# Local q and k loaded as rows of nine tokens, transposed by token pairs, and another order of the attention parts

## The chip, the cores and the metric

The kernel runs on one core of a Trainium2 chip. The metric is the device time of one execution in microseconds (us); less is better. The engines are TensorE (PE, with PEld for its weight loads), VectorE (DVE), ScalarE (ACT), GpSimd (POOL) and SyncE (SP), which issues all the DMAs here. TensorE's clock has two levels, 1.2 and 2.4 GHz; the profile gives the granted clock as a share of the upper one, so 0.50 is 1.2 GHz and 1.00 is 2.4 GHz.

## The reference

Three layers are chained, in fp32 (the MLP weights arrive as 64-bit floats).

```python
# attention: B=4, H=8, S=576, D=64; heads 0-3 local, heads 4-7 strided
rel = pos[:, None] - pos[None, :]
mask_local   = (rel >= 0) & (rel < 32)
mask_strided = (rel >= 0) & (pos[None, :] % 32 == pos[:, None] % 32)
attn = softmax(where(mask, q @ k.T / 8, -1e9)) @ v
x = attn.transpose(0, 2, 1, 3).reshape(2304, 512)
# soft mixture of 8 experts, 4 slots each: w1 (8,512,1024), w2 (8,1024,512)
logits = x @ phi
slot_in = softmax(logits, axis=0).T @ x
slot_out = relu(slot_in @ w1) @ w2          # expert by expert
x = softmax(logits, axis=1) @ slot_out
# MLP: w_in (512,2048), w_out (2048,512)
h = relu(x @ w_in)
out = (h * h) @ w_out
```

## The kernel before, in words

**Stages.** The attention part works on 16 units (`units`, L340): one batch and one pair of heads each, in the order of heads (0,1), (4,5), (2,3), (6,7), so that even units are local and odd units strided. After each four units (one batch) the logits and a running sum of the slot inputs are made (`L`, `R1`, `R2`, `R3`). `st_end` (L815) closes the attention stage. Then come the expert layers (`layer1` L1025, `layer2` L1048), in which 64 weight blocks of 512 KB are used, and then the MLP, whose inner product (L1229) fills the rest of the time.

**Parts of a unit.** `ld` (L368) loads q and k of a unit into one of NR = 3 raw buffers; `lv` (L392) loads v, and for a local unit `vs` (L407) copies v shifted by a block with two POOL copies (L410). `Tk` and `Tq` (`st_T`, L496) transpose k and q on PE into PSUM banks; `k` (L532) and `q` (L518) copy them out of the banks, q with the scale. `S` (L545) makes the scores, `s` (L583) subtracts the maximum on DVE, `e` (L608) takes the exponential on ACT, `n` (L612) normalises strided units, `PT` (L624) transposes the probabilities, `p` (L638) copies them out, `A` (L655) multiplies with v, `a` (L679) copies that out, `X` (L701) transposes the result and `x` (L711) copies it out.

**Order.** `PIPE` (L30) lists the parts of one iteration by hand, one list for even and one for odd units; a token's number is the lag (`A-1` is the part A of the unit before). `emit` (L921) walks through it. PE, ACT, DVE and POOL keep that order (`pin`, L100), one queue each. SP is not pinned: it issues a DMA in an order that the scheduler chose, each once its buffer is free, but a weight's DMA stays behind the last q/k load that was emitted before it (`pace`, L115).

**Local q and k before.** A local unit's q (and k) is loaded by three DMAs (L379 twice, L390): four tiles of 128 tokens for each of two heads and a rest of 64 tokens. Each token is a piece of 64 floats, 256 B. PE makes four transposes (L501) and one product with 64 columns of the identity (L503); the banks then hold tokens in order, and q leaves them by one ACT instruction (L525), k by two ACT copies of 64 partitions (L537, recorded at the helper's line L488). A strided unit's q and k come in pieces of 1024 B and 512 B (L385, L390).

**Weights.** `fetch` (L266) starts loads of expert and MLP weights into a ring of RING = 27 slots of 512 KB, and later into the 16 parts of the attention's own memory (`space`) as `give` (L299) hands them over when a unit's part was the last one to use it. The token `ft` starts `PACE` (L34) of them: 1 in an even and 2 in an odd iteration of the first half, 4 in an even and 0 in an odd one of the second half, 28 in all. `cv` converts one fetched w_in block. When all of `space` is given, `fetch` starts whatever still fits.

**Filling products.** `F1` and `DRAIN` (L25) put products without a use on PE (`fill_last`, L148, recorded at L153), one instruction each; `KEEP` does so in `st_end` (L824).

**Copies.** `ON_ACT` (L35) says which of a part's copies go to ACT (1) or DVE (0); for `n`, 2 means POOL.

Of the kernel before, what the change touches and what calls it, by code (L numbers as in the profile page):

```python
# [12 lines left out]
ALU = mybir.AluOpType  # L13
# [7 lines left out]
NA = 16  # L21
SPARE = 0
AHEAD = 4
KEEP = (4, 0, 0, 8, 0)
DRAIN = dict(S0=0, PT1=0, A1=3, X1=4, PT0=1, A0=1)  # L25
LATE = 3

PIPE = (  # L30
    "PT-1 p-1 lv+0 S+0 x-3 Tk+1 ft s+0 Tq+1 L-2 R2 vs+0 R3 ld+3 q+1 X-2 e+0 R1 n+0 cv F1 ld+4 A-1 lv+1 x-2 k+1 F1 F1 F1 a-1".split(),
    "PT-1 p-1 S+0 s+0 cv Tq+1 ft e+0 n+0 Tk+1 A-1 L-2 a-1 R2 k+1 vs+0 R1 X-2 q+1 R3".split(),
)
PACE = (1, 2, 4, 0)  # L34
ON_ACT = dict(kL=(1, 1), kS=(1, 1), pL=1, pS=(0, 0), xL=0, xS=1, aS=(1, 1, 1, 0), q=1, n=2)  # L35

@with_exitstack
def kernel(
# [119 lines left out]
    def flat(ps):  # L158
        return ps.rearrange("p b c -> p (b c)")
# [183 lines left out]
    ends = {}  # L343
    raws = {}
    for u in range(NU - NR, NU):
        raws[u % NR] = [part(128, 8 * D) for _ in range(2)] + [part(128, 2 * D)]
        ends["T", u] = at[0]
    qTl, kTl = part(128, S), part(128, 2, 32 + S)
    ends["S", NU - 2] = at[0]
# [13 lines left out]
    def local(u):  # L363
        return units[u][1] < 2

    raw = {}

    def load(u):  # L368
        if u >= NU:
            return  # L370
        b, p = units[u]
        raw[u] = raws[u % NR]
        r = raw[u][2]
        for n, src in ((1, k), (0, q)):
            i = src[b, 2 * p:2 * p + 2]
            m = raw[u][n]
            if local(u):
                for h in range(2):
                    nc.sync.dma_start(  # L379
                        out=m.rearrange("p (t h d) -> p t h d", h=2, d=D)[:, :, h],  # L380
                        in_=i[h, 0:512].rearrange("(t p) d -> p t d", p=128),
                    )
                o, i = r[64 * n:64 * n + 64].rearrange("p (h d) -> p h d", h=2), i[:, 512:576].rearrange("h p d -> p h d")
            else:
                nc.sync.dma_start(  # L385
                    out=m.rearrange("p (h x) -> p h x", h=2),
                    in_=i[:, 0:512].rearrange("h (p r) d -> p h (r d)", r=4),
                )
                o, i = r[64 * n:64 * n + 64], i[:, 512:576].rearrange("h (p e) d -> p h (e d)", e=2)
            pace[0] = nc.sync.dma_start(out=o, in_=i)  # L390
# [16 lines left out]
    def shift_v(u):  # L407
        if local(u):
            for h in range(2):
                nc.gpsimd.tensor_copy(  # L410
                    vL[64 * h:64 * h + 32, 1:18, h, 0:D], vL[64 * h + 32:64 * h + 64, 0:17, h, 0:D]
                )

# [51 lines left out]
    nc.vector.tensor_copy(masks, ms)  # L465
    for e in range(2):
        nc.vector.memset(kTs[ts(e, 64), :, 1 - e], 0.0)
    for h in range(2):
        nc.vector.memset(vL[ts(h, 64), :, 1 - h], 0.0)
    for h in range(2):  # L470
        nc.vector.memset(Ts[ts(h, 64), :, 2 - 2 * h:4 - 2 * h], 0.0)
    for t in (vS, Ps):
        behind(nc.gpsimd.memset(t, 0.0), last_diag)
    load_v(1)
# [2 lines left out]
    for t in El:  # L477
        behind(nc.gpsimd.memset(t[:, 192:256], 0.0), last_diag)
    shift_v(0)
    nc.gpsimd.tensor_copy(phi4[:, :, 1:4], phi4[:, :, 0:1].to_broadcast([128, KD, 3, NS]))  # L480
    nc.vector.tensor_reduce(
        out=sub2, in_=ident.rearrange("p (i c) -> p c i", c=2), axis=AX.X, op=ALU.add
# [11 lines left out]
        return ps  # L494

    def st_T(ps, u, n):  # L496
        m, r = raw[u][n], raw[u][2]
        pf = flat(ps)
        w = 128 if local(u) else 256
        for t in range(4):  # L500
            nc.tensor.transpose(out=pf[:, w * t:w * t + 128], in_=m[:, ts(t, 128)], identity=ident)  # L501
        if local(u):
            nc.tensor.matmul(out=pf[:, 512:576], lhsT=r, rhs=ident[:, ts(n, 64)], start=True, stop=True)  # L503
            return
        for h in range(2):
            nc.tensor.matmul(  # L506
                out=ps[:, h].rearrange("c (j x) -> c x j", j=2)[:, 128:144],
                lhsT=r, rhs=ident[:, ts(n, 64)].rearrange("k (p h) -> k h p", h=2)[:, h],
                start=True, stop=True,
            )  # L510

    def blocks(ps):
        return flat(ps).rearrange("c (n x) -> c n x", n=4)[:, :, 0:144]

    def st_Tq(u):
        st_T(hold("q", u), u, 0)

    def st_q(u):  # L518
        ps = held.pop(("q", u))
        if local(u):  # L520
            o, i = qTl, flat(ps)[:, 0:S]
        else:
            o, i = qTs, blocks(ps)
        if ON_ACT["q"]:
            nc.scalar.activation(out=o, in_=i, func=AF.Copy, scale=scale)  # L525
        else:
            nc.vector.tensor_scalar(out=o, in0=i, scalar1=scale, scalar2=None, op0=ALU.mult)

    def st_Tk(u):
        st_T(hold("k", u), u, 1)  # L530
# [1 line left out]
    def st_k(u):  # L532
        ps = held.pop(("k", u))
        i = blocks(ps)
        if local(u):
            for h in range(2):
                copy(ON_ACT["kL"][h], kTl[ts(h, 64), h, 32:32 + S], flat(ps)[ts(h, 64), 0:S])  # L537
        else:
            for e in range(2):
                copy(  # L540
                    ON_ACT["kS"][e], kTs[ts(e, 64), :, e].rearrange("c (b y) i -> c b y i", y=8),
                    i[ts(e, 64)].rearrange("c b (i y) -> c b y i", y=8),
                )

# [67 lines left out]
    def st_n(u):  # L612
        if local(u):
            return
        P = Pe.rearrange("p n (w s) -> p n w s", s=2)
        sm = ap_.tile([128, 8, 2], F32, tag="sm", name="sm", bufs=2)
        nc.vector.tensor_reduce(out=sm, in_=P.rearrange("p n w s -> p n s w"), axis=AX.X, op=ALU.add)
        nc.vector.tensor_scalar(out=sm, in0=sm, scalar1=1e-9, scalar2=None, op0=ALU.add)
        nc.vector.reciprocal(out=sm, in_=sm)
        (nc.gpsimd if ON_ACT["n"] == 2 and u < NU - 1 else nc.vector).tensor_tensor(  # L620
            out=P, in0=P, in1=sm[:, :, None, :].to_broadcast([128, 8, 18, 2]), op=ALU.mult
        )

# [14 lines left out]
    def st_p(u):  # L638
        pf = flat(held.pop(("p", u)))
        if local(u):  # L640
            copy(ON_ACT["pL"], Tl[:, 0:S], pf[:, 0:S])
        else:
            i = pf[:, 0:512].rearrange("p (n w) -> p n w", w=32)[:, :, 0:18]
            for h in range(2):
                r = ts(h, 64)
                if ON_ACT["pS"][h]:
                    for s in range(2):
                        nc.scalar.activation(out=Ts[r, :, 2 * h + s], in_=i[r], func=AF.Copy, scale=sub2[r, s:s + 1])
                else:
                    nc.vector.tensor_tensor(  # L650
                        out=Ts[r, :, 2 * h:2 * h + 2], in0=i[r, :, None, :].to_broadcast([64, 16, 2, 18]),
                        in1=sub2[r, None, :, None].to_broadcast([64, 16, 2, 18]), op=ALU.mult,
                    )
# [25 lines left out]
    def st_a(u):  # L679
        ps = held.pop(("a", u))  # L680
        if local(u):
            x = xNs[u] = xNb[:, u % 5]
            pv = flat(ps)[:, 122:772].rearrange("p (n e) -> p n e", e=65)
            den = ap_.tile([128, 10], F32, tag="den", name="den", bufs=2)
            nc.vector.tensor_scalar(out=den, in0=pv[:, :, D], scalar1=1e-9, scalar2=None, op0=ALU.add)
            nc.vector.reciprocal(out=den, in_=den)
            nc.vector.tensor_tensor(
                out=x.rearrange("p t (h d) -> p (t h) d", h=2), in0=pv[:, :, 0:D],
                in1=den[:, :, None].to_broadcast([128, 10, D]), op=ALU.mult,
            )  # L690
        else:
            xT = xTs[u] = xTb[u % 4]
            for h in range(2):
                for x in range(2):
                    copy(
                        ON_ACT["aS"][2 * h + x],
                        xT[ts(h, 64), 0:S].rearrange("c (i x k n) -> c x i k n", x=2, k=2, n=4)[:, x],
                        ps[ts(x, 64), :, 0:288].rearrange("c k (h i n) -> c h i k n", h=2, n=4)[:, h],
                    )
# [11 lines left out]
    def st_x(u, act=None):  # L711
        pf = flat(held.pop(("x", u)))
        if local(u):
            xT = xTs[u] = xTb[u % 4]
            copy(ON_ACT["xL"], xT[:, 0:S], pf[:, 0:S])
        else:
            x = xNs[u] = xNb[:, u % 5]
            copy(ON_ACT["xS"] if act is None else act, x, pf[:, 0:640].rearrange("p (t f) -> p t f", f=128))

    lps = {}  # L720

# [199 lines left out]
    def emit(u, token):  # L921
# [362 lines left out]
```

## Time and profile before

| what | us |
|---|---|
| median of 3 runs (413.55 to 416.15) | 415.74 |
| the profiled execution, whole | 418.53 |
| its span, first to last instruction | 416.8 |
| attention stage, to the first expert product (L1030) | 147.9 |
| expert layers, to the first product of the slots' sum (L1076) | 181.7 |

Times within the trace count from the span's start. The profiled execution lasted 1.7 us more than its span and 2.8 us more than the median. Over the span PE was busy 93%, DVE 58%, ACT 54%, POOL 22%.

### The profile page before, as it was taken

The page shows a single profiled execution, that of the slowest core. Times are in us where ns is not written, and L with a number is a line of the kernel's source. Part 1 is how long each engine was busy: PE and PEld are TensorE (multiplying, and loading weights), DVE is VectorE, ACT ScalarE, POOL GpSimd, SP SyncE. Part 2 cuts the span into 40 slices and gives each one's busy share as a digit, 9 for nine tenths or more (in the row PEclk, how much of TensorE's full clock was granted, in tenths as well). Part 3 has the DMA queues.
Part 4 walks back from the last instruction along what each step waited for, and adds up shares of the span by engine and source line. Part 5 has one row for each costly group of instructions (what it writes and reads, how often), then busy time and mean ns, then how long its engine had stood idle before and what let it go on. Part 6 is the DMA issues. An engine that isn't in the chain of part 4 may idle for free.

```text
span 416.8 us, 9152 instructions
## 1 busy us (share of the span) xinstructions
PE 387.3 (93%) x3654; PEld 302.3 (73%) x3654; DVE 242.6 (58%) x453; ACT 226.7 (54%) x459; POOL 90.8 (22%) x128
## 2 busy tenths in 40 slices
PE   6887798889699899999999999999999999999996
PEld 3776576777587645467788887888887888878884
DVE  6565547765265561138866564867657776745434
ACT  3452627536345220039778686666666676666760
POOL 6302211112022020035600252111414103420000
PEclk9998979999799999999999999999999999999999
DMA  6898898998999999997212131221000000003033
GB/s 153 234 251 227 215 227 300 210 293 203 274 384 270 395 333 417 417 417 309 87 64 102 51 103 58 95 101 50 2 0 1 2 0 2 1 0 153 37 116 151
DMA packets 52203, 69.88 MB, mean 168 GB/s; under 512 B 31744, under 2 KB 37120, under 8 KB 52160
## 3 DMA queue, kind: packets, MB, share of 16 engines
q1 hardware_dynamic: 52160, 69.29, 52.2%
q8 instruction: 29, 0.48, 0.5%
q14 instruction: 14, 0.11, 0.1%
HBM read 64.55 MB, written 4.72 MB: 166 GB/s over the span
## 4 chain that ended last, share of the span: by engine, by line
PE 73%; DMA 9%; DVE 5%; POOL 4%; ACT 3%; SPq 3%; issue 2%; POOLq 0%; DVEq 0%; ACTq 0%
PE banks L1229 43%; DMA space<-in_v_dram 6%; PE banks L1060 4%; PE banks L1190 4%; PE banks L1030 3%; PE banks L501 2%; DMA w<-in_moe_w_dram 2%; PE banks L554 2%; PE banks L1120 2%; PE banks L665 1%; PE banks L673 1%; POOL w L1105 1%; PE banks L728 1%; PE banks L734 1%; POOL space L410 1%
## 5 line engine op out<-in xcount | busy, mean ns | idle before, releaser
L1229 PE MATMUL banks<-w 128*128 128x512 f32 x864 | 218.3, 394 | 1.6 <-POOL w L1105 1.2
L1229 PEld LDWEIGHTS banks<-w 128*128 128x128 f32 x864 | 159.3, 188 | 37.2 <-POOL w L1105 2.9
L1206 DVE TENSOR_TENSOR w<-r,w 128x384 fp32r<-128x384 f32 (+1 forms) x97 | 57.8, 598 | 72.4 <-ACT w L1205 72.3
L1197 ACT ACTIVATE r<-banks 128x384 f32<-128x384 f32 (+1 forms) x96 | 47.0, 490 | 53.0 <-PE banks L1190 43.6
L1203 ACT ACTIVATE r<-r 128x384 f32<-128x384 f32 (+1 forms) x96 | 50.3, 524 | 3.0
L1205 ACT CAST w<-r 128x384 fp32r<-128x384 f32 (+1 forms) x97 | 49.5, 510 | 4.1 <-DVE r L1202 0.5
L488 ACT COPY space<-banks 64x576 f32<-64x576 f32 (+2 forms) x64 | 34.8, 543 | 19.5 <-PE banks L153 12.2
L220 POOL TENSOR_SCALAR nm<-w 128x512 f32<-128x512 f32 x28 | 23.5, 843 | 63.0 <-DMA w<-in_moe_w_out_dram 31.9
L1244 DVE TENSOR_TENSOR part<-banks,part 128x512 f32<-128x512 f32 (+1 forms) x55 | 34.9, 673 | 2.4 <-PE banks L1229 2.3
L410 POOL COPY space<-space 32x1088 f32<-32x1088 f32 x16 | 17.5, 1096 | 80.9 <-DMA space<-in_v_dram 57.6
L1104 POOL CAST w<-wf 128x512 fp32r<-128x512 f32 x16 | 11.8, 740 | 94.8 <-PE banks L1229 37.2
L1190 PE MATMUL banks<-cT,A 128*128 128x384 f32 x96 | 32.0, 335 | 0.0
L501 PE MATMUL banks<-ident,space 128*128 128x128 f32 x128 | 21.9, 297 | 1.6 <-DMA space<-in_q_dram 1.6
L224 DVE SCALAR_TENSOR_TENSOR nm<-w,nm 128x512 uint32<-128x512 uint32 x32 | 22.3, 696 | 1.1
L223 DVE TENSOR_SCALAR nm<-nm 128x512 uint32<-128x512 uint32 x32 | 14.6, 457 | 12.5 <-POOL nm L220 8.7
L1105 POOL TENSOR_TENSOR w<-wf,w 128x512 fp32r<-128x512 f32 x16 | 21.4, 1339 | 1.4
L525 ACT ACTIVATE space<-banks 128x576 f32<-128x576 f32 x16 | 10.4, 651 | 20.1 <-PE banks L506 15.9
L1190 PEld LDWEIGHTS banks<-cT,A 128*128 128x128 f32 x96 | 18.0, 188 | 3.9 <-ACT r L1197 0.2
L488 DVE COPY space<-banks 128x576 f32<-128x576 f32 (+1 forms) x16 | 9.7, 608 | 17.3 <-ACT space L488 13.5
L501 PEld LDWEIGHTS banks<-ident,space 128*128 128x128 f32 x128 | 15.7, 159 | 4.7 <-POOL w L437 2.5
L665 PE MATMUL banks<-space 128*32 128x130 f32 x288 | 13.0, 294 | 5.6 <-POOL space L410 3.7
L665 PEld LDWEIGHTS banks<-space 128*32 128x32 f32 x288 | 9.5, 116 | 7.7 <-POOL space L410 4.7
(186 smaller groups left out, 450.4 us busy)
## 6 DMA issues: line engine op xcount, KB each, us to landing
w<-in_moe_w_dram SPq DMA_DIRECT2D x48, 512.0 KB, 7.3
w<-in_moe_w_in_dram SPq DMA_DIRECT2D x16, 512.0 KB
space<-in_moe_w_dram SPq DMA_DIRECT2D x16, 512.0 KB, 7.4
w<-in_moe_w_out_dram SPq DMA_DIRECT2D x16, 512.0 KB, 6.6
space<-in_v_dram SPq DMA_DIRECT2D x32, 144.0 KB, 7.5
out_dram<-part SPq DMA_DIRECT2D x17, 256.0 KB, 2.0
space<-in_k_dram SPq DMA_DIRECT2D x16, 128.0 KB, 2.9
space<-in_q_dram SPq DMA_DIRECT2D x16, 128.0 KB, 2.6
```

The lines of the kernel that those rows point to most:

```text
L220: nc.gpsimd.tensor_scalar(out=m, in0=hf, scalar1=2.0 ** -112, scalar2=1.0, op0=ALU.mult, op1=ALU.mult)
L488: return (nc.scalar.copy if act else nc.vector.tensor_copy)(out=out, in_=in_)
L501: nc.tensor.transpose(out=pf[:, w * t:w * t + 128], in_=m[:, ts(t, 128)], identity=ident)
L665: nc.tensor.matmul(out=pv[c, n // 4] if n < 18 else pv[c, 4].rearrange("p (h e) -> p h e", h=2), lhsT=w, rhs=i, start=True, stop=True, til ...
L1105: nc.gpsimd.tensor_tensor(out=lo, in0=r, in1=hi.bitcast(F32), op=ALU.subtract)
L1190: nc.tensor.matmul(out=ps[:, 0:HB], lhsT=A4[c][:, ts(f % QF, 128)], rhs=cT4[:, c0:c0 + HB], start=True, stop=True)
L1197: nc.scalar.activation(out=r[:, cuts[0]], in_=ps[:, cuts[0]], func=AF.Relu)
L1203: nc.scalar.activation(out=r[:, cuts[0]], in_=r[:, cuts[0]], func=AF.Square)
L1205: nc.scalar.copy(out=gh[:, x], in_=r[:, x])
L1206: nc.vector.tensor_tensor(out=gl[:, x], in0=r[:, x], in1=gh[:, x].bitcast(F32), op=ALU.subtract)
L1229: nc.tensor.matmul(out=acc[t], lhsT=a[:, ts(t, 128)], rhs=wo[f][:, ts(w, 512)], start=(first and k == 0), stop=(last and k == 2),)
L1244: nc.vector.tensor_tensor(out=pt[:, cs], in0=acc[t][:, cs], in1=pt[:, cs], op=ALU.add)
```

## The change

A local unit's q (and k) is loaded by one DMA, each of 128 partitions taking nine consecutive tokens of one head, one piece of 2304 B. PE transposes two tokens at a time (four transposes of 128 columns and one of 64); tokens then lie out of order in the banks, even ones of nine on partitions 0 to 63 and odd ones on 64 to 127, and four copies of 64 partitions ("quarters", two of 320 and two of 256 elements) put them in order, writing every ninth element. The order of the parts, the fetch counts, the engines of the copies (now apart for the first two units, `_b`, and the last two, `_e`) and the filling products change too; `n`'s product goes from POOL to DVE for units 2 to 13, the first unit's `Tk k Tq q` are emitted ahead, and four clearings of memory go from DVE to POOL.

```diff
-KEEP = (4, 0, 0, 8, 0)
-DRAIN = dict(S0=0, PT1=0, A1=3, X1=4, PT0=1, A0=1)
+KEEP = (4, 0, 0, 8, 3)
+DRAIN = dict(S0=3, PT1=0, A1=4, X1=8, PT0=0, A0=0)
 PIPE = (
-    "PT-1 p-1 lv+0 S+0 x-3 Tk+1 ft s+0 Tq+1 L-2 R2 vs+0 R3 ld+3 q+1 X-2 e+0 R1 n+0 cv F1 ld+4 A-1 lv+1 x-2 k+1 F1 F1 F1 a-1".split(),
-    "PT-1 p-1 S+0 s+0 cv Tq+1 ft e+0 n+0 Tk+1 A-1 L-2 a-1 R2 k+1 vs+0 R1 X-2 q+1 R3".split(),
+    "vs+0 Tq+1 PT-1 x-3 p-1 q+1 S+0 s+0 R2 ft L-2 Tk+1 cv k+1 R1 X-2 e+0 R3 x-2 A-1 ld+3 ld+4 n+0 lv+1 F1 a-1".split(),
+    "S+0 s+0 Tk+1 e+0 cv k+1 PT-1 Tq+1 p-1 R2 R3 A-1 ft vs+0 n+0 L-2 X-2 a-1 q+1 lv+1 R1".split(),
 )
-PACE = (1, 2, 4, 0)
-ON_ACT = dict(kL=(1, 1), kS=(1, 1), pL=1, pS=(0, 0), xL=0, xS=1, aS=(1, 1, 1, 0), q=1, n=2)
+PACE = (0, 2, 4, 0)
+ON_ACT = dict(kL=(1, 1, 1, 1), qL=(1, 1, 1, 1), kS=(1, 1), pL=0, pS=(0, 0), xL=0, xS=1, aS=(1, 0, 1, 1), q=1, n=0, vs=(0, 0), kL_b=(1, 1, 1, 1), qL_b=(0, 0, 0, 1), kL_e=(0, 1, 0, 1), qL_e=(0, 0, 1, 1), ...)
@@ load
-            if local(u):
-                for h in range(2):
-                    nc.sync.dma_start(
-                        out=m.rearrange("p (t h d) -> p t h d", h=2, d=D)[:, :, h],
-                        in_=i[h, 0:512].rearrange("(t p) d -> p t d", p=128),
-                    )
-                o, i = r[64 * n:64 * n + 64].rearrange("p (h d) -> p h d", h=2), i[:, 512:576].rearrange("h p d -> p h d")
...
+            if local(u):
+                todo_ = [(raw[u][:, ts(n, 9 * D)], i.rearrange("h (x r) d -> (h x) (r d)", r=9))]
@@ constants
-    for h in range(2):
-        nc.vector.memset(vL[ts(h, 64), :, 1 - h], 0.0)
-    for h in range(2):
-        nc.vector.memset(Ts[ts(h, 64), :, 2 - 2 * h:4 - 2 * h], 0.0)
...
     shift_v(0)
+    for h in range(2):
+        nc.gpsimd.memset(vL[ts(h, 64), :, 1 - h], 0.0)
+    for h in range(2):
+        nc.gpsimd.memset(Ts[ts(h, 64), :, 2 - 2 * h:4 - 2 * h], 0.0)
@@ st_T
+        if local(u):
+            m = raw[u][:, ts(n, 9 * D)]
+            for w in range(5):
+                c = min(128, 9 * D - 128 * w)
+                nc.tensor.transpose(out=pf[0:c, ts(w, 128)], in_=m[:, 128 * w:128 * w + c], identity=ident)
+            return
@@ st_q, st_k
+    def quarters(t, ps):
+
+        for h in range(2):
+            for e in range(2):
+                o = (t[ts(h, 64), h] if len(t.shape) == 3 else t[ts(h, 64)]).rearrange("c (x r) -> c r x", r=9)
+                i = flat(ps)[ts(e, 64), 0:640].rearrange("c (w h x) -> c h w x", w=5, h=2)
+                yield 2 * h + e, o[:, e:9:2], i[:, h, 0:5 - e]
-            o, i = qTl, flat(ps)[:, 0:S]
+            todo_ = [(on("qL", u)[n], o, i) for n, o, i in quarters(qTl, ps)]
-            for h in range(2):
-                copy(ON_ACT["kL"][h], kTl[ts(h, 64), h, 32:32 + S], flat(ps)[ts(h, 64), 0:S])
+            for n, o, x in quarters(kTl[:, :, 32:32 + S], ps):
+                copy(on("kL", u)[n], o, x)
@@ the loop over the units
+    for token in ("Tk+1", "k+1", "Tq+1", "q+1"):
+        emit(-1, token)
     for u in range(-1, NU + 3):
         for token in PIPE[u % 2]:
             emit(u, token)
```

## Rows read from the trace of the kernel before

**Rows 1.** The page's 40 slices, GB/s that the DMA engines moved.
```profile
GB/s 153 234 251 227 215 227 300 210 293 203 274 384 270 395 333 417 417 417 309 87 64 102 51 103 58 95 101 50 2 0 1 2 0 2 1 0 153 37 116 151
```
**Rows 2.** Windows: length, busy us of five engines, granted clock, DMA share, GB/s.
```profile
0.00:10.00 10.00, 6.28 (x21) 3.45 (x21) 6.02 (x18) 2.75 (x4) 6.22 (x27) 1.00 0.66 152
10.50:98.20 87.70, 74.67 (x1381) 60.99 (x1381) 52.17 (x103) 41.83 (x84) 17.06 (x27) 0.94 0.92 240
98.20:147.90 49.70, 42.96 (x736) 34.72 (x730) 26.78 (x63) 20.37 (x48) 6.84 (x7) 0.93 1.01 322
147.90:177.00 29.10, 29.10 (x362) 13.37 (x365) 8.29 (x14) 4.11 (x6) 2.23 (x4) 1.00 0.99 388
51.30:58.10 6.80, 6.80 (x61) 5.51 (x63) 2.69 (x7) 1.88 (x6) 0.00 (x0) 0.50 0.99 306
109.30:116.10 6.80, 5.56 (x107) 4.91 (x108) 0.79 (x2) 1.82 (x4) 2.13 (x2) 0.50 1.11 274
```
**Rows 3.** The chain that ended last: start us, us, what.
```profile
10.50 2.04 PE banks L554 x33
...
23.07 8.96 DMA space<-in_v_dram
...
34.48 2.37 PE banks L665 x35
...
147.90 7.04 PE banks L1030 x64
...
181.69 0.84 PE banks L1076 x8
```
**Rows 4.** Waits from 0 to 150 us: waiting line, what ended it, us, times, longest.
```profile
PE banks L673 <- DMA space<-in_v_dram: 3.9, 2, 3.7
PE banks L665 <- POOL space L410: 3.7, 3, 1.4
...
PE banks L634 <- POOL space L620: 2.2, 2, 1.3
...
PE banks L629 <- ACT space L488: 2.0, 3, 1.0
...
PE banks L665 <- DMA space<-in_v_dram: 1.9, 2, 1.4
```
**Rows 5.** Timeline of SP's DMA issues: start us, us, line, transfer, count.
```profile
0.81 0.99 SPq L379 DMA_DIRECT2D space<-in_k_dram  x2
...
3.79 0.61 SPq L390 DMA_DIRECT2D space<-in_q_dram  x1
...
148.93 20.66 SPq L120 DMA_DIRECT2D w<-in_moe_w_dram  x21
```
**Rows 6.** The page's DMA issues: transfer, count, KB each, median us to landing.
```profile
w<-in_moe_w_dram SPq DMA_DIRECT2D x48, 512.0 KB, 7.3
```
**Rows 7.** Groups by shape, 0 to 180 us: busy us, mean ns, idle before.
```profile
L501 PE MATMUL banks<-ident,space 128*128 128x128 f32 x128 | 21.9, 297 | 1.6 <-DMA space<-in_q_dram 1.6
L488 ACT COPY space<-banks 64x576 f32<-64x576 f32 x32 | 20.2, 631 | 6.9 <-PE banks L503 6.4
...
L525 ACT ACTIVATE space<-banks 128x576 f32<-128x576 f32 x16 | 10.4, 651 | 20.1 <-PE banks L506 15.9 <-DVE space L589 4.0
...
L488 ACT COPY space<-banks 64x288 f32<-64x288 f32 x24 | 9.5, 394 | 12.4 <-PE banks L153 12.2
...
L503 PE MATMUL banks<-ident,space 128*128 128x64 f32 x32 | 5.7, 263 | 0.0
...
L153 PE MATMUL banks<-maskl,identb 128*128 128x384 bf16 x17 | 4.6, 327 | 0.0
...
L488 DVE COPY space<-banks 64x288 f32<-64x288 f32 x8 | 3.7, 461 | 15.7 <-ACT space L488 13.5 <-PE banks L734 2.1
...
L447 DVE MEMSET space<- 64x32 f32 x2 | 0.2, 85 | 0.1
...
L449 DVE MEMSET space<- 64x18 f32 x2 | 0.1, 73 | 0.0
```

More of the change, by code (lines that the diff above doesn't have):

```diff
@@ L23 @@
 AHEAD = 4
-KEEP = (4, 0, 0, 8, 0)
-DRAIN = dict(S0=0, PT1=0, A1=3, X1=4, PT0=1, A0=1)
+KEEP = (4, 0, 0, 8, 3)
+DRAIN = dict(S0=3, PT1=0, A1=4, X1=8, PT0=0, A0=0)
 LATE = 3
 PIPE = (
-    "PT-1 p-1 lv+0 S+0 x-3 Tk+1 ft s+0 Tq+1 L-2 R2 vs+0 R3 ld+3 q+1 X-2 e+0 R1 n+0 cv F1 ld+4 A-1 lv+1 x-2 k+1 F1 F1 F1 a-1".split(),
-    "PT-1 p-1 S+0 s+0 cv Tq+1 ft e+0 n+0 Tk+1 A-1 L-2 a-1 R2 k+1 vs+0 R1 X-2 q+1 R3".split(),
-)
-PACE = (1, 2, 4, 0)
-ON_ACT = dict(kL=(1, 1), kS=(1, 1), pL=1, pS=(0, 0), xL=0, xS=1, aS=(1, 1, 1, 0), q=1, n=2)
+    "vs+0 Tq+1 PT-1 x-3 p-1 q+1 S+0 s+0 R2 ft L-2 Tk+1 cv k+1 R1 X-2 e+0 R3 x-2 A-1 ld+3 ld+4 n+0 lv+1 F1 a-1".split(),
+    "S+0 s+0 Tk+1 e+0 cv k+1 PT-1 Tq+1 p-1 R2 R3 A-1 ft vs+0 n+0 L-2 X-2 a-1 q+1 lv+1 R1".split(),
+)
+PACE = (0, 2, 4, 0)
+ON_ACT = dict(kL=(1, 1, 1, 1), qL=(1, 1, 1, 1), kS=(1, 1), pL=0, pS=(0, 0), xL=0, xS=1, aS=(1, 0, 1, 1), q=1, n=0, vs=(0, 0), kL_b=(1, 1, 1, 1), qL_b=(0, 0, 0, 1), kL_e=(0, 1, 0, 1), qL_e=(0, 0, 1, 1), kS_b=(1, 1), kS_e=(0, 0), pL_b=0, pL_e=0, pS_b=(0, 0), pS_e=(0, 0), xL_b=0, xL_e=0, xS_b=1, xS_e=0, aS_b=(1, 1, 1, 1), aS_e=(1, 1, 1, 0), q_b=0, q_e=1, n_b=2, n_e=2, vs_b=(0, 0), vs_e=(0, 0))
 @with_exitstack
@@ L345 @@
     for u in range(NU - NR, NU):
-        raws[u % NR] = [part(128, 8 * D) for _ in range(2)] + [part(128, 2 * D)]
+        raws[u % NR] = part(128, 18 * D)
         ends["T", u] = at[0]
@@ L364, in local, with on @@
         return units[u][1] < 2
+    def on(what, u):
+        return ON_ACT[what + ("_b" if u < 2 else "_e" if u >= NU - 2 else "")]
     raw = {}
@@ L372, in load @@
         raw[u] = raws[u % NR]
-        r = raw[u][2]
         for n, src in ((1, k), (0, q)):
             i = src[b, 2 * p:2 * p + 2]
-            m = raw[u][n]
             if local(u):
-                for h in range(2):
-                    nc.sync.dma_start(
-                        out=m.rearrange("p (t h d) -> p t h d", h=2, d=D)[:, :, h],
-                        in_=i[h, 0:512].rearrange("(t p) d -> p t d", p=128),
-                    )
-                o, i = r[64 * n:64 * n + 64].rearrange("p (h d) -> p h d", h=2), i[:, 512:576].rearrange("h p d -> p h d")
-            else:
[L385 to L390, printed above, removed]
+                todo_ = [(raw[u][:, ts(n, 9 * D)], i.rearrange("h (x r) d -> (h x) (r d)", r=9))]
+            else:
+                todo_ = [(
+                    raw[u][:, ts(n, 8 * D)].rearrange("p (h x) -> p h x", h=2),
+                    i[:, 0:512].rearrange("h (p r) d -> p h (r d)", r=4),
+                ), (
+                    raw[u][64 * n:64 * n + 64, 16 * D:18 * D],
+                    i[:, 512:576].rearrange("h (p e) d -> p h (e d)", e=2),
+                )]
+            for o, i in todo_ if n else reversed(todo_):
+                pace[0] = nc.sync.dma_start(out=o, in_=i)
     def load_v(u):
@@ L409, in shift_v @@
             for h in range(2):
-                nc.gpsimd.tensor_copy(
+                (nc.vector if on("vs", u)[h] else nc.gpsimd).tensor_copy(
                     vL[64 * h:64 * h + 32, 1:18, h, 0:D], vL[64 * h + 32:64 * h + 64, 0:17, h, 0:D]
@@ L496, in st_T @@
     def st_T(ps, u, n):
-        m, r = raw[u][n], raw[u][2]
         pf = flat(ps)
-        w = 128 if local(u) else 256
+        if local(u):
[4 more added lines that the diff above has]
+            return
+        m, r = raw[u][:, ts(n, 8 * D)], raw[u][:, 16 * D:18 * D]
         for t in range(4):
-            nc.tensor.transpose(out=pf[:, w * t:w * t + 128], in_=m[:, ts(t, 128)], identity=ident)
-        if local(u):
-            nc.tensor.matmul(out=pf[:, 512:576], lhsT=r, rhs=ident[:, ts(n, 64)], start=True, stop=True)
-            return
+            nc.tensor.transpose(out=pf[:, 256 * t:256 * t + 128], in_=m[:, ts(t, 128)], identity=ident)
         for h in range(2):
@@ L520, in st_q @@
         if local(u):
-            o, i = qTl, flat(ps)[:, 0:S]
+            todo_ = [(on("qL", u)[n], o, i) for n, o, i in quarters(qTl, ps)]
         else:
[L523 to L527, printed above, removed]
+            todo_ = [(on("q", u), qTs, blocks(ps))]
+        for act, o, i in todo_:
+            if act:
+                nc.scalar.activation(out=o, in_=i, func=AF.Copy, scale=scale)
+            else:
+                nc.vector.tensor_scalar(out=o, in0=i, scalar1=scale, scalar2=None, op0=ALU.mult)
     def st_Tk(u):
@@ L540, in st_k @@
                 copy(
-                    ON_ACT["kS"][e], kTs[ts(e, 64), :, e].rearrange("c (b y) i -> c b y i", y=8),
+                    on("kS", u)[e], kTs[ts(e, 64), :, e].rearrange("c (b y) i -> c b y i", y=8),
                     i[ts(e, 64)].rearrange("c b (i y) -> c b y i", y=8),
@@ L619, in st_n @@
         nc.vector.reciprocal(out=sm, in_=sm)
-        (nc.gpsimd if ON_ACT["n"] == 2 and u < NU - 1 else nc.vector).tensor_tensor(
+        (nc.gpsimd if on("n", u) == 2 and u < NU - 1 else nc.vector).tensor_tensor(
             out=P, in0=P, in1=sm[:, :, None, :].to_broadcast([128, 8, 18, 2]), op=ALU.mult
@@ L640, in st_p @@
         if local(u):
-            copy(ON_ACT["pL"], Tl[:, 0:S], pf[:, 0:S])
+            copy(on("pL", u), Tl[:, 0:S], pf[:, 0:S])
         else:
@@ L645, in st_p @@
                 r = ts(h, 64)
-                if ON_ACT["pS"][h]:
+                if on("pS", u)[h]:
                     for s in range(2):
@@ L695, in st_a @@
                     copy(
-                        ON_ACT["aS"][2 * h + x],
+                        on("aS", u)[2 * h + x],
                         xT[ts(h, 64), 0:S].rearrange("c (i x k n) -> c x i k n", x=2, k=2, n=4)[:, x],
@@ L714, in st_x @@
             xT = xTs[u] = xTb[u % 4]
-            copy(ON_ACT["xL"], xT[:, 0:S], pf[:, 0:S])
+            copy(on("xL", u), xT[:, 0:S], pf[:, 0:S])
         else:
             x = xNs[u] = xNb[:, u % 5]
-            copy(ON_ACT["xS"] if act is None else act, x, pf[:, 0:640].rearrange("p (t f) -> p t f", f=128))
+            copy(on("xS", u) if act is None else act, x, pf[:, 0:640].rearrange("p (t f) -> p t f", f=128))
     lps = {}
```

## The prediction

> **What bounds the kernel now.** I read the windows by stage first. From 10.5 to 98.2 us (the first twelve units) PE is busy 74.7 of 87.7 us and the DMA engines 0.92 of the time, yet they move only 240 GB/s; from 98.2 to 147.9 us their share is 1.01 at 322 GB/s; in the expert layers 0.99 at 388 GB/s [rows 2], where the slices reach 417 [rows 1]. So two resources are nearly full up to 177 us, and the first stretch gets little out of its DMA time. Next the chain: one v load takes 8.96 us of it at 23.07, and the product with v starts only at 34.48, at 2.37 us for its 35 instructions [rows 3]. Then the waits: that product stood 3.7 us for POOL's shift of v and 1.9 us for v itself, its strided sibling 3.9 us (3.7 in one piece) [rows 4]. Behind such stalls the granted clock fell to 0.50, that is to 1.2 GHz: from 51.3 to 58.1 and from 109.3 to 116.1 us; over the two attention stretches it means 0.94 and 0.93 [rows 2]. From 147.9 to the end of the experts at 181.7 us [rows 3] PE never stands. The last expert weight is issued at 148.93 + 20.66 = 169.6 us at the latest [rows 5] and lands some 7.3 us later [rows 6], near 177: the weights arrive just before their use, so PE and DMA end this stage together. The MLP behind it is left alone by the change; I take it to move as a block.
>
> **The change, part by part.** *Transfers.* Local q and k are 8 units x 2 x 294,912 B = 4.72 MB. In the first 10 us 1.52 MB moved in 6.6 us of DMA time [rows 2]; by the loads that were issued then, 0.59 MB of q and k and 0.29 MB of v went in 256 B pieces and 0.59 MB in larger ones. If the larger ones ran at 417 GB/s (1.4 us), the small ones ran at 0.88 MB / 5.2 us = 170 GB/s; if all ran alike, at 230. Then 4.72 MB costs 20.5 to 27.8 us now. Pieces of 2304 B are in no row; at 417 GB/s they cost 11.3 us, at worst they stay as they are. I take 417, because 512 KB weights reach it, and a saving of 14 us (0 to 16), 1.8 us a local unit. SP issues two DMAs in place of six: the first unit's six began at 0.81 and the last at 3.79 [rows 5].
>
> *Copies.* By the rows a copy of 64x576 on ACT takes 631 ns and one of 64x288 394 ns, on DVE 461; the q copy takes 651 ns [rows 7]. Two quarters of 320 and two of 256 elements are four of 288 in the mean: 4 x 394 = 1.58 us for q and as much for k, 3.15 in place of 651 + 2 x 631 = 1.91 us. That is 1.24 us more of ACT per local unit, 9.9 us over eight. ACT is busy 41.8 of 87.7 us there [rows 2], so the work fits; what matters is the latency. In the new order q's quarters stand behind k's on ACT, and between `Tq` and the next local `S` PE has A, X, a strided `Tq` and `PT`: some 25 instructions of the L501 kind and 35 of A, at least 3 us. I take 0 to 7.4 us in the six pairs to 98.2, and 1. PE makes five transposes for four and an L503 product; at 297 and 263 ns [rows 7] this is nothing.
>
> The quarters write every ninth float. The nearest row that writes far apart is the column of ones, 64x18 at a distance of 520 B: 73 ns against 85 for 64x32 in one piece [rows 7]. At a slope of (85 - 73)/14 = 0.86 ns an element that is no penalty, but it is DVE and a clearing; for ACT no row shows it. The Trainium skill (SBUF — State Buffer, section Door 1: The DMA port swizzle) says that SBUF is accessed in lines of 16 bytes and that each step to a new line costs extra, which speaks against this change; it gives no figure. Were each element to take twice its time, the sum would grow by about 0.8 ns x 288 x 8 = 1.9 us of ACT per local unit; the row disagrees for DVE, and this weighs in the slower rival.
>
> *Waits in the first stretch.* v is issued after A as before, but behind fewer and cheaper transfers, and the order gives it more of an iteration: the 3.7 + 1.9 + 0.2 us of waits [rows 4] go, 5.8 (bounds 0 and 5.8; a wait that stays in part is why the total below is cut). The clock's mean of 0.94 over 87.7 us [rows 2] means 10.5 us at the half level, so up to 5.2 us lost; I take 4. The strided transposes stood 2.2 us for `n` on POOL and the local ones 2.0 for ACT [rows 4]; both parts move, and I take back 2 of 4.2. Three filling products fewer in each even iteration, 18 in six pairs, at 4.6/17 = 0.27 us [rows 7]: 0 to 4.9, I take 2.5. Together 14.3, less 1 for the copies and less 1.3 for waits that the new order makes instead: 12 (3 to 16). What is late next is PE itself: 74.7 us of work in this stretch.
>
> *The start.* The first `S` begins at 10.5 us [rows 3]. With two DMAs in place of six for q and k, the transposes can begin near 4.5, but four quarters follow, split between ACT and DVE. I take 2 us (0 to 4). The clearings that go to POOL are needed only by the first A; they lie beside PE's work.
>
> *The weights.* Counting `PACE`: in the first eight iterations 8 weights in place of 12; in the second half the same 16. Whatever the attention gains, the stream from unit 12 on then holds four weights more: 4 x 524,288 B / 417 GB/s = 5.0 us. It also holds unit 14's load, 1.8 us cheaper. This stretch, from 98.2 to 177, was at a DMA share of 1.0 [rows 2] and runs as long as its bytes: 78.8 + 5.0 - 1.8 = 82 us. Bounds: 72 (had the stream waited for memory rather than for the engines) and 86.
>
> *The end.* The last expert weight then lands at 98.2 - 2 - 12 + 82 = 166.2 in place of 177, and the experts end 4.7 us behind it as now, with 0.3 for PE that has been waiting. PE alone would be ready earlier (below), so the weights set the end. The filling products added at the end (nine instructions net, up to 0.27 us each) lie under that. Sum: -2 - 12 + 3.2 + 0.3 = -10.5 us; 418.5 - 10.5 = 408.0 for the profiled execution, which is 2.8 us above the median of the runs: **405.2 us**.
>
> **The rivals.** *The weights do not limit.* If the stream after unit 12 was held by memory, PE sets the end: -2 - 12, and in the second stretch the 3.7 us for v [rows 4], 2.8 us at the half clock (half of 5.56 busy [rows 2]) and 0.5 for other waits: -21, that is 394.7. For it: PE did not stand once after 147.9, and SP's stretches of waiting for freed memory. Against: the DMA share of 1.0. *The order brings its own stalls.* The v waits move to other parts, and the first stretch gains only 3 us: -2 - 3 + 3.2 + 0.3 = -1.5, that is 414.2; the saved DMA time becomes idle DMA time. For it: PE's share there is already 85%, and `PT`, `p`, `A` of a local unit now stand close together. Against: the waits in rows 4 are nearly all for v. *Slower: the quarters stand in the path.* If PE's cover between `Tq` and `S` is shorter than the quarters' 1.58 us behind k's 1.58, each local unit is late by the 1.24 us added: +9.9 - 2 for the start, that is 423.6. It decides from the point where the score product waits for the q copy in every pair; twice the price per element would do it. Against it: a cover of over 3 us and the row of the ones. That the change does not do what it says would show in the count of packets; I see no way for it.
>
> **How the numbers follow.** Forecast 0.61, with its own range of 399 to 411; weights do not limit 0.17; own stalls 0.14; quarters in the path 0.08. A measurement of this kernel tells about 1% (4.2 us) from no change: faster means under 411.6, slower over 419.9. Faster: 0.61 x 0.97 + 0.17 + 0.14 x 0.25 = 0.80; slower 0.08; within 1%: 0.12. The range reaches to the first and second rival: 394 to 414.5.
>
> **What would show it.** Right: packets under 512 B fall by 18,432 (8 units x 2 x 1,152); the DMA share up to unit 12 falls to about 0.8; the v waits ahead of A are under 1 us in all; the twelfth unit's transposes start near 84; the expert products show waits for weights, and end near 171. Wrong: idle PE in front of `S` with the q copy as its releaser; a DMA share of 0.9 in the first stretch; or expert layers without a wait, which is the first rival.

## The result and the profile after

The change made the kernel slower: 421.61 us (median of 16 runs, 416.66 to 424.52) against 417.56 us for the kernel before (16 runs, 411.35 to 420.75). Ratios and their intervals, here and below, compare fast executions, those within 1.5% of their kernel's quickest (here 11, median 420.57 us, and 8, median 415.09 us): 1.013, 1.010 to 1.016; over all 32 executions it is 1.010. A gain of 2.5% was forecast.

The two profiled executions are nearly equal, 418.35 and 418.53 us: the changed kernel's lies 3.3 us below its median, that of the kernel before 1.0 us above. So the traces below show where some 10 us of expected gain stayed, and not the last 1.3%. Two more kernels with the same copies (e9 and e13, below) were profiled at 418.4 and 418.7 us of span, where the changed kernel has 416.6.

What became of the loads and of the clock is read from the pages and from the windows of the changed kernel (answering to [rows 2]; length, busy us of PE, PEld, DVE, ACT, POOL, granted clock, DMA share, GB/s); of the two lines on packets the first is of the kernel before. The first window ends where the transposes of unit 12 begin, 91.2 us in place of 98.2.

```profile
DMA packets 52203, 69.88 MB, mean 168 GB/s; under 512 B 31744, under 2 KB 37120, under 8 KB 52160
DMA packets 35305, 69.85 MB, mean 168 GB/s; under 512 B 12800, under 2 KB 18176, under 8 KB 35264
```

```profile
10.50:91.20 80.70, 68.10 (x1341) 55.77 (x1341) 53.68 (x104) 56.51 (x100) 17.12 (x26) 0.93 0.79 224
91.20:146.90 55.70, 46.81 (x732) 37.44 (x728) 35.38 (x77) 23.53 (x52) 4.39 (x4) 0.88 1.03 324
```

The DMA engines did get their relief: a share of 0.79 in the first twelve units, where it was 0.92. But PE is busy 68.1 of 80.7 us, 84%, no larger a share than before (85%), and ACT, which had 41.8 us of work in its 87.7, has 56.5 in 80.7. The waits of PE from 0 to 150 us answer to [rows 4]:

```profile
PE banks L644 <- ACT space L535: 3.8, 3, 1.3
PE banks L675 <- DVE space L487: 3.3, 5, 2.3
PE banks L153 <- ACT space L487: 3.2, 2, 1.8
PE banks L719 <- ACT space L487: 3.1, 3, 1.1
PE banks L738 <- ACT space L487: 2.6, 2, 1.4
PE banks L505 <- DMA space<-in_q_dram: 2.1, 1, 2.1
```

No wait for v of 0.4 us or more is left. In their place PE waits for ACT at L487 (k's quarters) and L535 (q's), eight times by 1.0 to 1.4 us, 9.5 us in all: the strided `X` (L719), the logits (L738) and the strided `PT` (L644). The waits of the local `A` for `p` on DVE (L675) and of the filling products (L153) are not the quarters': they stand in e1 (below) too, at 2.7 and 3.2 us. The groups by shape answer to [rows 7] and say why:

```profile
L487 ACT COPY space<-banks 64x320 f32<-64x320 f32 x14 | 10.2, 727 | 3.4 <-PE banks L501 3.0
L487 ACT COPY space<-banks 64x256 f32<-64x256 f32 x16 | 9.9, 616 | 1.3 <-DVE space L487 1.0
L487 ACT COPY space<-banks 64x288 f32<-64x288 f32 x25 | 9.8, 393 | 14.9 <-PE banks L153 8.9 <-DVE space L487 5.8
...
L535 ACT ACTIVATE space<-banks 64x320 f32<-64x320 f32 x13 | 9.6, 742 | 4.6 <-DVE space L537 4.3
...
L535 ACT ACTIVATE space<-banks 64x256 f32<-64x256 f32 x14 | 8.8, 626 | 2.3 <-DVE space L537 1.9
...
L537 DVE TENSOR_SCALAR space<-banks 64x320 f32<-64x320 f32 x3 | 2.1, 717 | 0.0
```

A quarter costs 616 to 742 ns on ACT, while a copy of 288 elements that is not spaced out still costs 393. Four quarters of k are 2 x 727 + 2 x 616 = 2.69 us, four of q 2 x 742 + 2 x 626 = 2.74: 5.4 us of ACT for each local unit, where 1.91 were needed before and 3.15 were forecast. The chain that ended last, from 60 to 69 us (start us, us, what; answering to [rows 3]), goes straight through them:

```profile
61.01 0.45 ACT space L620
61.46 0.01 issue
61.48 0.74 ACT space L487
62.22 0.01 issue
62.23 0.63 ACT space L487
62.87 0.01 issue
62.88 0.73 ACT space L487
63.62 0.01 issue
63.63 0.62 ACT space L487
64.25 0.04 issue
64.30 0.77 PE banks L719 x5
65.06 0.44 PE banks L505 x4
65.50 0.38 PE banks L507 x4
65.88 0.03 ACTq L535
65.91 0.52 ACT space L535
66.43 0.01 issue
66.44 0.63 ACT space L535
67.07 0.04 issue
67.12 0.67 PE banks L644 x4
```

Read it from the top: the exponential of a strided unit (L620), then the four quarters of k, then five transposes that had waited for the last of them, two groups of PE work, the rest of q's quarters, and the strided `PT`. The whole of k's copies and half of q's are the path.

### The profile page after: what moved, and what is told of

Its sections match the earlier page's. It is cut to its first block, busy times and chain, and to the rows that moved or that the text cites. A ratio compares the mean times of both kernels' runs of the same rounds, so it can differ in the third digit from the quotient of the medians.

```text
span 416.6 us, 9069 instructions
## 1 busy us (share of the span) xinstructions
PE 384.4 (92%) x3620; PEld 300.0 (72%) x3620; DVE 252.6 (61%) x472; ACT 245.9 (59%) x482; POOL 90.7 (22%) x126
## 4 chain that ended last, share of the span: by engine, by line
PE 70%; DVE 11%; ACT 7%; POOL 3%; issue 2%; POOLq 0%; DVEq 0%; ACTq 0%
PE banks L1241 43%; ACT space L487 4%; PE banks L1202 4%; PE banks L1072 3%; PE banks L1042 3%; DVE space L487 2%; DVE space L660 2%; PE banks L1132 2%; PE banks L719 1%; POOL w L1117 1%; PE banks L738 1%; PE banks L744 1%; DVE nm L224 1%; PE banks L683 1%; DVE mx L598 1%
## 5 line engine op out<-in xcount | busy, mean ns | idle before, releaser
L487 ACT COPY space<-banks 64x288 f32<-64x288 f32 (+3 forms) x69 | 38.8, 562 | 31.0 <-PE banks L153 8.9
L535 ACT ACTIVATE space<-banks 64x256 f32<-64x256 f32 (+2 forms) x34 | 23.0, 677 | 7.5 <-DVE space L537 6.3
L487 DVE COPY space<-banks 128x576 f32<-128x576 f32 (+3 forms) x27 | 18.2, 675 | 6.7 <-ACT space L487 2.1
L660 DVE TENSOR_TENSOR space<-banks,sub 64x576 f32<-64x576 f32 x16 | 12.1, 755 | 11.7 <-ACT xNb L487 9.8
L675 PE MATMUL banks<-space 128*32 128x130 f32 x288 | 12.0, 304 | 3.3 <-DVE space L487 3.3
L501 PE MATMUL banks<-ident,space 128*128 128x128 f32 (+1 forms) x80 | 13.3, 305 | 1.0 <-ACT space L487 1.0
L675 PEld LDWEIGHTS banks<-space 128*32 128x32 f32 x288 | 9.3, 121 | 6.2 <-DVE space L487 4.9
```

Source lines behind the costliest of these rows:

```text
L487: return (nc.scalar.copy if act else nc.vector.tensor_copy)(out=out, in_=in_)
```

## The experiments

All ratios are to the kernel before, run on the same chip at the same time. Thirteen kernels ran.

**The price of the spaced write.** e1 writes the same elements in one run:

```diff
-                o = (t[ts(h, 64), h] if len(t.shape) == 3 else t[ts(h, 64)]).rearrange("c (x r) -> c r x", r=9)
+                o = t[ts(h, 64), h] if len(t.shape) == 3 else t[ts(h, 64)]
+                o = o[:, 320 * e:320 + 256 * e].rearrange("c (r x) -> c r x", x=64)
                 i = flat(ps)[ts(e, 64), 0:640].rearrange("c (w h x) -> c h w x", w=5, h=2)
-                yield 2 * h + e, o[:, e:9:2], i[:, h, 0:5 - e]
+                yield 2 * h + e, o, i[:, h, 0:5 - e]
```

> The changed kernel, but each quarter is written as one dense run instead of to every ninth float, so q and k stand in a wrong order of tokens (the same number of copies, elements, products and DMAs). Theory 1 (the spaced writes double the copies, and the doubled copies stand in PE's path): the ACT quarters fall from 727 and 616 ns to about 420 and 370, PE's waits for them ahead of the strided PT, X and L (1.0 to 1.3 us each, some 12 us in all up to 99 us) mostly go, the expert layers begin 8 to 14 us earlier, and the time is 0.97 to 0.985 of before. Theory 2 (the new order of the parts makes its own stalls, whatever a copy costs): the waits stay, 1.005 to 1.015 of before. Theory 3 (the weights set the end of the expert layers, so that a faster attention gains nothing): attention ends earlier, but the expert products wait for weights, 1.00 to 1.01.

Measured: 408.22 us, 0.983 (0.977 to 0.990). The quarters take 418 and 368 ns:

```profile
L487 ACT COPY space<-banks 64x256 f32<-64x256 f32 x16 | 5.9, 368 | 0.9 <-DVE space L487 0.6
L487 ACT COPY space<-banks 64x320 f32<-64x320 f32 x14 | 5.8, 418 | 3.6 <-PE banks L501 3.2
```

PE's waits for them ahead of `X`, the logits and the strided `PT` are gone from the list, unit 12 begins at 77.3 us and the expert layers at 135.2 in place of 146.9. Theory 1 holds on each of its points, and the whole loss and more comes back. Attention's gain at unit 12 is 20.9 us against the kernel before, though, and at its end only 12.7: something else takes 8 us in the last units (below).

e2 puts the tokens in the right place and only exchanges the loops of the copy:

```diff
-                o = (t[ts(h, 64), h] if len(t.shape) == 3 else t[ts(h, 64)]).rearrange("c (x r) -> c r x", r=9)
-                i = flat(ps)[ts(e, 64), 0:640].rearrange("c (w h x) -> c h w x", w=5, h=2)
-                yield 2 * h + e, o[:, e:9:2], i[:, h, 0:5 - e]
+                o = (t[ts(h, 64), h] if len(t.shape) == 3 else t[ts(h, 64)]).rearrange("c (x r) -> c x r", r=9)
+                i = flat(ps)[ts(e, 64), 0:640].rearrange("c (w h x) -> c h x w", w=5, h=2)
+                yield 2 * h + e, o[:, :, e:9:2], i[:, h, :, 0:5 - e]
```

> The changed kernel with the two loops of a quarter's copy exchanged: for each group of nine tokens it writes the five (or four) floats that lie two apart, and reads the bank 128 floats apart. Theory 1 in the form that a write is dear where each float lands in another 16 bytes: most writes share their 16 bytes with the one before, so the quarters fall to about 420 and 370 ns, and the time is 0.97 to 0.985 of before. Should any write that is not dense cost double, or the far reads cost as much: quarters of 600 ns or more and 1.005 to 1.02. Theory 2: no change of time even if the quarters become short.

Measured: 410.25 us, 0.988 (0.982 to 0.994), a little above the range of theory 1. The groups by shape of e2 show ACT's quarters at the price of dense ones, or nearly:

```profile
L487 ACT COPY space<-banks 64x256 f32<-64x256 f32 x16 | 6.7, 418 | 0.9 <-DVE space L487 0.6
L487 ACT COPY space<-banks 64x320 f32<-64x320 f32 x14 | 6.1, 438 | 3.6 <-PE banks L501 3.2
L535 ACT ACTIVATE space<-banks 64x256 f32<-64x256 f32 x14 | 6.0, 428 | 2.4 <-DVE space L537 2.0
L535 ACT ACTIVATE space<-banks 64x320 f32<-64x320 f32 x13 | 5.8, 447 | 5.4 <-DVE space L537 5.1
```

So it is neither the count of the copies nor the spaced reading of a bank (here 128 floats apart) that costs; it is the order in which SBUF is written.

e10 measures the price by distance, a different one in each local unit:

```diff
+    STEPS = {0: 9, 2: 1, 4: 2, 6: 3, 8: 4, 10: 5, 12: 6, 14: 8}
...
+                    yield 2 * h + e, o[:, 0:64 * s].rearrange("c (x r) -> c r x", r=s)[:, 0:min(s, 4)], i[:, 0:min(s, 4)]
```

> A measurement of the price alone: in the changed kernel the quarters of unit 0 are written as there (every ninth float), those of local units 2, 4, 6, 8, 10, 12 and 14 with a distance of 1, 2, 3, 4, 5, 6 and 8 floats, 256 elements each (128 at 2, 192 at 3), so q and k are incomplete. If a write costs double where each float lands in another 16 bytes: on ACT some 370 ns at 1, 265 at 2, between 315 and 470 at 3, and 620 from 4 on, the same at 4, 5, 6, 8 and 9. If the price grows with the distance: a rise from 4 to 9.

The timeline of ACT in e10 (start us, us, line, shape, count; one row is k's four quarters with the short gaps between them) at distances of 1, 2, 3 and 4 floats:

```profile
19.21 1.54 ACT L487 COPY space<-banks 64x256 f32<-64x256 f32 x4
...
30.30 1.17 ACT L487 COPY space<-banks 64x128 f32<-64x128 f32 x4
...
41.00 1.76 ACT L487 COPY space<-banks 64x192 f32<-64x192 f32 x4
...
55.98 2.56 ACT L487 COPY space<-banks 64x256 f32<-64x256 f32 x4
```

One instruction took 367 ns in the mean at a distance of 1, 273 at 2 (half the elements), 422 at 3 (three quarters of them) and 620 at 4; at 5, 6 and 8 it is 623, 618 and 614. With the 157 ns that a copy costs before its first element ([rows 7]: 631 and 394 ns for 576 and 288 elements give 0.82 ns each and 157 over), that is 0.82, 0.91, 1.38 and 1.81 ns an element, and level from 4 floats on. The price follows the 16 bytes, not the distance. The Trainium skill (SBUF — State Buffer, section Door 1: The DMA port swizzle) says that SBUF has lines of 16 bytes, and that an access is at full rate where two in a row fall into one line. This kernel agrees: at 8 bytes, two writes to a line, an element takes 0.91 ns on ACT, near the 0.82 of a dense one, and at 16 bytes 1.81, 2.2 times as long. On DVE, 320 elements took 717 ns against 476 in e1 and 256 took 626 against 426; less the 226 ns that the two dense times leave before the first element, that is about twice the time for each element.

**The order alone and the layout alone.** e3 is the kernel before with the new loads, transposes and quarters; e4 is the changed kernel with the old ones. Their diffs are the parts of the diff above, `load` to `st_k` in e3, all else in e4.

> The kernel before (its order, fetch counts, filling products and engines) with the new layout alone: one DMA for q and one for k, transposes by pairs of tokens, four spaced quarters each, all on ACT. Theory 1: 5.4 us of ACT instead of 1.9 in each local unit, in an order not made for it: 1.01 to 1.04 of before, with S waiting for q. Theory 2 (the order is what costs): 0.985 to 1.00, since the cheaper loads are had without the order.

> The changed kernel (its order, fetch counts, filling products and engines) with the old layout: loads in 256 B pieces, four transposes and a product, q in one copy and k in two. Theory 1: the copies are 1.9 us again but the DMA engines are full again: 0.985 to 1.005 of before, with waits for v. Theory 2: the stalls stay, 1.01 to 1.02.

Measured: e3 435.33 us, 1.051 (1.044 to 1.059); e4 419.71 us, 1.011 (1.005 to 1.016). In e3 the scores and the strided `PT` stand for q's quarters (waits, 0 to 150 us, in an execution of 440.34 us, the slowest of its four):

```profile
PE banks L644 <- ACT space L535: 12.3, 3, 4.3
PE banks L564 <- ACT space L535: 11.2, 4, 5.4
```

So the new layout with spaced quarters costs 5% in the old order (more than the 1 to 4% of theory 1), and only 1.3% together with the new one. The new order is itself no gain with the old layout: in e4 unit 12 begins at 87.5 us, 10.7 earlier than before, yet the experts begin at 146.6. Its last units wait 4.8 us for v and spend some 17 us at the half clock (13.7 of them in one piece), at a DMA share of 0.99. So e4's time lies in the range of theory 2, while its trace shows the full DMA engines and the waits for v of theory 1. Short copies in the old order were not run: how much of e2's gain needs the new order is open.

**What is late next.** In the last units of e2, v of unit 13 stands behind weights. Its chain:

```profile
93.02 10.91 DMA w<-in_moe_w_dram
...
103.94 10.46 DMA space<-in_v_dram
...
114.54 1.22 PE banks L683 x32
```

e5 keeps the weights that are emitted after v of unit 13 behind its load, e6 restores the old fetch count, e8 does both; e7 is e4 with the edit of e5; e11 is e8 with still more early weights (`PACE = (2, 2, 4, 0)`).

```diff
 # e5, in load_v
+        if u == 13:
+            pace[0] = ins
 # e6
-PACE = (0, 2, 4, 0)
+PACE = (1, 2, 4, 0)
```

> The kernel of e2_runs_of_token, and the weights that are emitted after v's load of unit 13 stay behind that load on SP. In e2 that v was issued at 101.7 us, 8 us after its buffer was free, landed at 114.4, and PE stood and cooled for it. Theory A (in the last units v stands behind weights in SP's queue, and this gives back what the first units gain): PE's waits for v go, attention ends 4 to 8 us earlier than 138.8, and the time is 0.975 to 0.985 of before. Theory B (the step of the prediction: the weights set the end of the expert layers): attention ends earlier, but the expert products then wait for weights and the time stays at 0.985 to 0.992.

> The kernel of e2_runs_of_token with the old fetch count in the first half (1 in an even iteration, 2 in an odd one), so four weights are loaded earlier. Theory B (the weights limit the end): 3 to 5 us faster than e2, 0.975 to 0.98 of before. Theory A (memory and v's place in the queue limit, not the number of early weights): within 2 us of e2, or slower if the four weights delay q, k or v in the first units.

> The kernel of e4_old_layout (new order, old loads and copies) with the weights behind v's load of unit 13. In e4 the first twelve units were 10 us faster than before, yet the experts began at 146.6, as before. Theory A: the last units lose their wait of 4.8 us for v and part of the 13.7 us at the half clock, and the time falls from 1.011 to about 0.99 of before. Theory B: no change, 1.005 to 1.015.

> Both: v of unit 13 ahead of the weights, and four weights more in the first half. Theory A with B behind it: with the wait for v gone the weights become the limit, so the four weights help here where they do not alone: 0.965 to 0.978 of before, faster than e5 by 2 to 5 us. Theory A alone: as e5.

> The kernel of e8 with eight weights more than the changed kernel in the first half (2 in each iteration) in place of four. If the weights' stream still sets the end: 1 to 4 us faster than e8, 0.972 to 0.981 of before. If loads of q, k and v now come late in the first units: as e8 or slower.

Measured: e5 407.98 us, 0.985 (0.982 to 0.989); e6 410.48, 0.989 (0.984 to 0.995); e7 417.81, 1.010 (1.005 to 1.015); e8 407.44, 0.982 (0.975 to 0.990); e11 414.96, 0.999 (0.994 to 1.004). Attention ended at 135.6, 135.6, 146.6, 135.1 and 140.5 us. Neither theory of e5 came as written: attention ended 3.2 us earlier than in e2, not 4 to 8, and the wait for v did not go but moved to unit 15 (3.6 us); and the expert products waited for weights 0.2 us at most. e6 took as long as e2, as theory A has it. In e7 the wait for v broke into three (4.5, 2.0 and 3.1 us) and nothing was gained, theory B's range. e8 missed its range and is as e5, the second outcome. Intervals of e2, e5, e6 and e8 overlap, so that e5 or e8 beats e2 is likely but not shown. Eight early weights are worse than four, the second outcome of e11: its chain runs through loads of k, of a w_in block, of q and of k from 9.7 to 37.8 us, unit 12 begins at 90.7 us where e8 has 88.0, and its attention is 5.4 us longer.

Early weights move more than transfers. In e8, as in the kernel before, all four conversions of w_in blocks (`cv`) lie ahead of unit 12; the changed kernel and e2 have three there. They stand on DVE in front of a local unit's `p`, and `A` waits 5.5 us for `p` in e8 (e2: 2.0). So unit 12 begins at 83.0 us in e2 and at 88.0 in e8, and the last four units take 55.8 and 47.1 us.

e9 makes e8's two edits on the spaced quarters:

> The changed kernel with its spaced quarters, and the two edits of e8 (v of unit 13 ahead of the weights, four weights more in the first half). If the doubled copies in PE's path set the changed kernel's time, the two edits, which were worth about 2.5 us on the short copies, change nothing that can be told: 1.005 to 1.018 of before. If the DMA queue set it: 0.99 to 1.00.

Measured: 420.19 us, 1.013 (1.008 to 1.018), as the change itself. The edits move time here too: unit 12 begins at 97.0 us in place of 91.2, and the last four units take 50.8 us in place of 55.7. With the long copies nothing of that is left at the end of attention (147.8 and 146.9 us), with the short ones 3.7 us (e8 and e2).

**DMA work taken away.** e12 (from e8) and e13 (from the changed kernel) leave v's loads of the later local units out:

```diff
+        if local(u) and u >= 2:
+            return
```

> The kernel of e8 without v's loads for the local units 2 to 14 (they use the first unit's v; 2.06 MB in 256 B pieces are not moved). If the DMA engines are what is late next once the copies are short: attention ends 4 to 9 us earlier than 135.1 and the time is 0.96 to 0.972 of before. If they are not: within 2 us of e8, 0.978 to 0.986.

> The changed kernel, its spaced quarters kept, without the same loads of v. If the doubled copies bound it and the DMA engines do not: within 3 us of the changed kernel, 1.004 to 1.016 of before. If DMA time still bounds it: 0.985 to 1.00.

Measured: e12 403.87 us, 0.973 (0.966 to 0.980); e13 419.47 us, 1.013 (1.007 to 1.019). In e12 attention ended at 133.0 us, 2.1 earlier than in e8 where 4 to 9 were expected, and its time misses the range by 0.001. The windows from 10.5 us to unit 12 and on to the end of attention, e8 first, then e13:

```profile
10.50:88.00 77.50, 67.07 (x1341) 54.99 (x1329) 56.62 (x107) 47.27 (x101) 17.77 (x26) 0.95 0.92 275
88.00:135.10 47.10, 40.75 (x727) 32.94 (x723) 32.41 (x74) 19.92 (x51) 4.41 (x4) 1.00 0.95 316
```

```profile
10.50:93.75 83.25, 69.74 (x1340) 56.95 (x1340) 52.39 (x104) 56.47 (x100) 16.59 (x25) 0.92 0.64 197
93.75:149.40 55.65, 46.82 (x731) 37.60 (x724) 35.30 (x77) 23.51 (x52) 4.38 (x4) 0.88 0.89 316
```

In e13 the DMA share of the first stretch falls to 0.64, unit 12 begins no earlier (93.75 us) and the time stays: the DMA engines do not bound the changed kernel. With short copies (e8) their share is 0.92 and 0.95, and e12's ratio lies 0.009 under e8's; the intervals overlap, so this half points to the DMA engines as what is late next without settling it.

## Why the prediction was wrong, step by step

**The step that failed is the copies.** "4 x 394 = 1.58 us for q and as much for k" was the price of the row for 288 elements; the quarters took 2.74 and 2.69 us. The doubling had been weighed, and turned down by the row of a clearing on DVE (18 elements at 520 B took 73 ns). The row was read rightly: the dense clearings of the same trace, 85 ns for 32 elements and 565 for 608, put 73 ns for 18. But a clearing was no stand-in for a copy: DVE's own spaced copies took 717 ns where dense ones took 476. The nearest row was not near, and the other price that was weighed, twice the time an element and 1.9 us more a local unit, was close: 2.2 times, and 5.43 - 3.15 = 2.28 us.

**Their place was wrong too.** The cover was counted between `Tq` and the next local `S`. PE stood there 1.8 us in all (L560 and L564, 0.9 each, for q's quarters); it stood more in front of `X`, the logits and the strided `PT`, released by the quarters' end, because k's quarters come behind a strided unit's exponential on ACT and q's behind k's. The 1 us that the sum allowed for six pairs (0 to 7.4) compares with 13.9 us that unit 12 loses between e1 (77.3) and the changed kernel (91.2). The copies account for most of the miss: 0.975 was forecast, 1.013 measured, and e1, with the copies near the price of the sum, has 0.983.

**The rest of the sum.** From the start to unit 12 the trace gains 7.0 us (14 forecast). From there to the slots' sum it loses 6.0 (3.5 forecast), and the MLP, taken to move as a block, is 0.8 us longer. In e1 the same three are a gain of 20.9, a loss of 9 and a loss of 0.9. So the last four units are the second thing that the sum had wrong: it reckoned them by the bytes of the stream, and in the trace they run at a clock of 0.88, with 13.7 us at the half level where the kernel before has 6.8.

**What held.** Packets under 512 B fell by 18,944 (18,432 forecast); the DMA share of the first stretch is 0.79 (forecast 0.8); the waits for v ahead of `A` are gone. With the copies near the forecast price, the first stretch gains what was forecast or more: from 98.2 to 83.0 us in e2 and 77.3 in e1, against -14. Part of that is one conversion and four weights that these two leave for later; with the old fetch count (e8) unit 12 begins at 88.0. The clock's gain did not come: 0.93 in the first stretch, 0.88 in the second.

**The start** was to gain 2 us and gained none. The first `S` again begins at 10.5 us: in the new order the strided `Tq` of unit 1 stands ahead of it and waited 2.1 us for its q (above), and then `S` waited 0.9 us for the quarters.

**The weights** were to set the end of the expert layers. They did not: attention's end and the first product of the slots' sum lie 33.8 us apart both before and after, and PE's waits for weights in between come to 0.7 us at most in the kernels with short copies and to 1.0 in e4. Expert layers without a wait were the prediction's sign for its first rival, whose 394.7 us did not come because the first stretch did not gain. "82 us from unit 12 to the last weight" was close in size (91.2 to 168.1, the last issue, and some 7 us to land, 84), but what came late by it was v in SP's queue (e2's chain), not the weights in the experts.

**The rival that won** is the slower one, quarters in the path, at 423.6 us; 1.013 of the 415.74 from which it was reckoned is 421.1. It had a chance of 0.08. Its mechanism was right, with the wait at three other products than the one it named; the twice dearer element was named there as the point from which it decides. Its number is luck: it adds 9.9 us of ACT and takes 2 off at the start, while by the traces the copies cost 13.9 us up to unit 12, the rest of the change gained 20.9, and the start nothing.

What stays open: in the traces the changed kernel is level with the kernel before, and the 1.3% is in the many runs; no profile shows that part by itself. The clock points to it: the changed kernel's 16 executions have a mean granted clock of 0.956 to 0.981, median 0.967, and the 40 of the kernel before that were run beside the experiments 0.967 to 1.000, median 0.986, where its profiled one has 0.979.

## What to carry to other kernels

Before trading small DMA pieces for a sorting copy, look at the order in which the copy writes: at a distance of 16 bytes or more between neighbours each fp32 element took about twice as long (2.2 times on ACT, 2.0 on DVE), and exchanging the loops so that near elements follow each other gives nearly all of it back, here 1.013 turned into 0.988 by three lines. A bound that is turned down by one row should be turned down by a row of the same kind of instruction. And count a longer copy's cover on the engine's whole queue: here the products that waited were not the ones that use the copy, but later ones that take its banks.

Of the kernels that leave nothing out e8 has the lowest median, 407.44 us, 0.982 (0.975 to 0.990) of the kernel before; e2, e5 and e6 are not told apart from it.

## What was not expected of the hardware

ACT writes a spaced fp32 at about 1.8 ns an element, the same from 16 to 36 bytes of distance, and DVE at about 1.5 (717 less 226 ns, for 320), while reading a bank at 512 bytes of distance, in runs of five or four, costs ACT 20 to 50 ns a copy at most (e2 against e1: 438 and 418 ns for 320 elements, 418 and 368 for 256; e2's writes are not dense either). A DVE clearing of 18 elements 520 bytes apart shows no such price.
